# Loading the queries' input in eight strided transfers in place of one, in a cached attention block

## The chip, the cores and the metric

The kernel runs on one core of a Trainium2 chip. The metric is the device time of one execution in microseconds; of several runs the median is given. A profile is one further execution, recorded instruction by instruction: its span runs from the first to the last recorded instruction, and its own device time is a little more than the span. A core has five instruction streams: TensorE (PE, whose weight loads are listed as PEld), VectorE (DVE), ScalarE (ACT), GpSimd (POOL) and SyncE (SP). SP computes nothing; it issues nearly all transfers between the device's memory and the on-chip memory. Sixteen DMA engines carry these out.

## The reference

A block of grouped-query attention with cached keys and values: 8 sequences (B), 4 new tokens each (Sq), 32 query heads in 8 groups that share a key and value head each, 2048 cached positions (Sk), head size 128, all in bf16.

```python
def reference(x, k_cache, v_cache, wq, wo):      # x: 8 x 4 x 512
    q = (x @ wq).reshape(B, Sq, Hq, Dh).transpose(0, 2, 1, 3)
    k = jnp.repeat(k_cache, rep, axis=1)         # caches: 8 x 8 x 2048 x 128
    v = jnp.repeat(v_cache, rep, axis=1)
    scores = jnp.einsum("bhqd,bhkd->bhqk", q, k) * (Dh ** -0.5)
    p = softmax(scores)
    o = jnp.einsum("bhqk,bhkd->bhqd", p, v)
    return o.transpose(0, 2, 1, 3).reshape(B, Sq, Hq * Dh) @ wo
```

x is 32 rows of 512 numbers, 32 KB in all; each cache is 32 MB, wq and wo 4 MB each.

## The kernel before

The caches are worked through in 16 units (NU) of four key heads of one sequence. A unit has a load of keys and one of values, 2 MB each, called K0 to K15 and V0 to V15 here (load_k, line 87; load_v, line 98; V15 is cut in two). Keys and values have three buffers each (KB and VB). So K3 can only be issued when the first keys have been used, that is turned by VectorE (turn_keys, line 136), and V3 when the first values have been multiplied on TensorE (values, line 290). The output weights wo follow the last values in six pieces (load_wo, line 103), in the buffer that held wq.

All these transfers are issued by SP, in the order in which the code names them: K0 (line 105), wq (line 106), x (line 107), then K1, K2, V0 by load_ready(0, 0), and inside the loop over the units K3, V1, K4, V2 and so on, each once its buffer is free. SP works through its instructions one by one: one that waits holds up all that stand behind it.

The framework that builds the program gives each transfer a semaphore that counts its completion. For transfers issued by SP and ACT there are eight of these, used in turn; they are called lanes 0 to 7 here. Where a lane has been used before and its earlier transfer isn't yet known to SP to have landed, the framework has SP wait for that before it issues the next one on the lane. In the kernel before, the lanes of the first issues are K0 0, wq 1, x 2, K1 3, K2 4, V0 5, K3 6, V1 7, and K4 starts again with lane 0. K3 waits for lane 0, since its buffer is that of K0.

Ahead of the loop x is turned by four transposes on TensorE (line 146, out of x_sb, into xtp) and copied (line 149); 16 matmuls with wq give the queries of the first half of the heads (line 156), which are scaled (line 167), turned (line 176) and spread into the block-diagonal q_bd (line 182). Line 130 and the two turnings of K0 (line 136) stand ahead of that on VectorE and don't need x.

A pass n of the loop turns the keys of unit n (not for n = 0, done ahead), multiplies them with q_bd (scores, line 205), spreads the probabilities of unit n-1 (lines 251 to 261), takes maxima (line 223) and exponentials (line 241) of unit n, and multiplies the probabilities of unit n-2 with its values (line 290). VectorE's order is written out by hand: the turning of K1 comes behind the maxima of unit 0, and so behind all work on x. At the end, the last products with wo (project, line 358) wait for the last piece of wo, and the output is copied and sent out by ACT and SP (lines 420 to 422).

Of the kernel before, what the change touches and what calls it, by code (L numbers as in the profile page):

```python
# [14 lines left out]
def kernel(  # L15
# [9 lines left out]
    nc = tc.nc  # L25
# [42 lines left out]
    x_sb = const.tile([T, D], BF16, name="x_sb")  # L68
# [35 lines left out]

    load_k(0)
    nc.sync.dma_start(wq_sb[:, :, :], wq.rearrange("(p r) n -> p r n", r=R))
    nc.sync.dma_start(x_sb[:, :], x.flatten_outer_dims())
    loads = [("k", 1)]
    for u in range(2, NU + 2):
        if u < NU:  # L110
# [342 lines left out]
```

## Time and profile before

| | us |
|---|---|
| median of 3 runs | 185.89 (185.8 to 186.16) |
| the profiled execution, device time | 185.75 |
| the profiled execution, span | 183.8 |
| busy in the span: PE / DVE / ACT / POOL | 122.7 / 119.6 / 77.6 / 59.1 |
| HBM read | 75.53 MB, 411 GB/s over the span |
| chain that ended last: DMA / DVE / PE | 59% / 25% / 9% |

The profile's page cuts the span into 40 slices of 4.6 us and prints for each the busy share of the engines and of the DMA engines in tenths, and the bytes moved. Its chain that ended last starts from the last instruction and goes back, at each step, to what released it. Its DMA rows give, for each group of issues, the size and the median time from the start of the issue on SP to landing. Views of the trace behind the page show the same for a tile, a line or a window of time; a window that holds one issue alone gives that issue's own time to landing. SP's rows in a timeline are the issues themselves, with the time that the issuing instruction took.

### The profile page before, as it was taken

The page shows a single profiled execution, that of the slowest core. Times are in us where ns is not written, and L with a number is a line of the kernel's source. Part 1 is how long each engine was busy: PE and PEld are TensorE (multiplying, and loading weights), DVE is VectorE, ACT ScalarE, POOL GpSimd, SP SyncE. Part 2 cuts the span into 40 slices and gives each one's busy share as a digit, 9 for nine tenths or more (in the row PEclk, how much of TensorE's full clock was granted, in tenths as well). Part 3 has the DMA queues.
Part 4 walks back from the last instruction along what each step waited for, and adds up shares of the span by engine and source line. Part 5 has one row for each costly group of instructions (what it writes and reads, how often), then busy time and mean ns, then how long its engine had stood idle before and what let it go on. Part 6 is the DMA issues. An engine that isn't in the chain of part 4 may idle for free.

```text
span 183.8 us, 2500 instructions
## 1 busy us (share of the span) xinstructions
PE 122.7 (67%) x932; PEld 79.6 (43%) x932; DVE 119.6 (65%) x156; ACT 77.6 (42%) x136; POOL 59.1 (32%) x127
## 2 busy tenths in 40 slices
PE   0000471639997887849596839496866987499982
PEld 0000130214664663626364625355553746269761
DVE  4180209796999989494958677676957695945210
ACT  2000203535575764907273634538382629084020
POOL 8800111515185351605151513233231405056000
PEclk9999998556999999997969987969997599969999
DMA  6999999999999999999999999999999999999980
GB/s 193 485 399 410 428 431 431 424 442 431 428 428 435 426 421 431 428 442 431 421 435 424 431 428 431 435 428 442 417 435 421 435 435 431 431 417 424 430 353 23
DMA packets 5914, 75.71 MB, mean 412 GB/s; under 512 B 688, under 2 KB 912, under 8 KB 1296
## 3 DMA queue, kind: packets, MB, share of 16 engines
q1 hardware_dynamic: 5856, 75.55, 96.8%
q8 instruction: 7, 0.11, 0.2%
q10 hardware_dynamic: 48, 0.02, 0.0%
q14 instruction: 3, 0.02, 0.0%
HBM read 75.53 MB, written 0.03 MB: 411 GB/s over the span
## 4 chain that ended last, share of the span: by engine, by line
DMA 59%; DVE 25%; PE 9%; SPq 2%; issue 1%; POOL 1%; ACT 1%
DMA k_sb<-in_k_cache_dram 39%; DVE kt L136 19%; DMA wo_sb<-in_wo_dram 11%; DMA x_sb<-in_x_dram 9%; PE s_ps L205 5%; DVE top L223 3%; PE o_ps L290 2%; PE psq L156 1%; SPq L98 1%; DVE swapped L215 1%; POOL q_bd L182 1%; DVE q_t L176 1%; SPq L103 1%; PE out_ps L358 1%; DVE less L229 1%
## 5 line engine op out<-in xcount | busy, mean ns | idle before, releaser
L136 DVE STREAM_TRANSPOSE kt<-k_sb 128x2048 f32<-128x2048 f32 x32 | 72.0, 2288 | 21.5 <-DMA k_sb<-in_k_cache_dram 21.5
L205 PE MATMUL s_ps<-kt,q_bd 128*64 128x512 bf16 x256 | 45.0, 483 | 38.5 <-DVE kt L136 35.4
L290 PE MATMUL o_ps<-v_sb,probs 128*128 128x256 bf16 x512 | 62.9, 285 | 0.0
L261 ACT COPY probs<-p_t 32x512 bf16<-32x512 bf16 x62 | 38.2, 615 | 54.6 <-DVE r_sb L279 53.4
L261 POOL COPY probs<-p_t 32x512 bf16<-32x512 bf16 x63 | 38.5, 612 | 58.8 <-DVE r_sb L279 56.4
L290 PEld LDWEIGHTS <-probs 128*128 128x128 bf16 x512 | 51.2, 102 | 14.5 <-issue 6.6
L205 PEld LDWEIGHTS <-q_bd 128*64 128x64 bf16 x256 | 17.1, 127 | 56.3 <-issue 24.7
L223 DVE TENSOR_REDUCE top<-s_ps 128x1 f32<-128x1024 f32 x16 | 19.6, 1223 | 16.1 <-PE s_ps L205 16.1
L241 ACT ACTIVATE s_sb<-s_ps,less 128x1024 bf16<-128x1024 f32 x16 | 22.3, 1397 | 10.6 <-DVE less L229 10.2
L215 POOL COPY l_swapped<-l_sb 64x1 f32<-64x1 f32 x32 | 5.8, 180 | 32.1 <-ACT s_sb L241 31.3
L306 ACT ACTIVATE o_sc<-o_ps,r_sb 64x128 f32<-64x128 f32 x28 | 10.1, 362 | 7.4 <-PE o_ps L290 6.7
L146 PE MATMUL xtp<-ident,x_sb 32*128 32x32 bf16 x4 | 0.3, 194 | 18.3 <-DMA x_sb<-in_x_dram 18.3
L251 DVE STREAM_TRANSPOSE p_t<-s_sb 128x512 f32<-128x512 f32 x16 | 11.0, 689 | 1.6 <-ACT s_sb L241 1.6
L167 ACT ACTIVATE q_nat<-psq 128x512 bf16<-128x512 f32 x2 | 1.2, 590 | 18.8 <-PE psq L156 18.8
L182 POOL COPY q_bd<-q_t 32x512 bf16<-32x512 bf16 x6 | 3.7, 624 | 16.6 <-DVE q_t L176 16.5
L313 PEld LDWEIGHTS o_t<-both,o_sc 128*128 128x128 f32 x32 | 5.2, 204 | 6.8 <-issue 5.1
L146 PEld LDWEIGHTS <-x_sb 32*128 32x128 bf16 x4 | 0.2, 113 | 18.3 <-DMA x_sb<-in_x_dram 18.3
L313 PE MATMUL o_t<-both,o_sc 128*128 128x64 f32 x32 | 7.2, 311 | 0.2 <-DVE o_sc L308 0.2
L129 POOL MEMSET probs<- 128x4096 bf16 x2 | 7.0, 3512 | 0.0
L215 DVE COPY swapped<-top 64x1 f32<-64x1 f32 x32 | 4.7, 148 | 0.8
L358 PE MATMUL out_ps<-wo_sb,oP 128*32 128x256 bf16 x64 | 4.6, 274 | 0.5 <-DMA wo_sb<-in_wo_dram 0.5
L308 DVE TENSOR_SCALAR o_sc<-o_ps,r_sb 64x128 f32<-64x128 f32 x4 | 1.4, 349 | 4.7 <-issue 3.0
(32 smaller groups left out, 39.3 us busy)
## 6 DMA issues: line engine op xcount, KB each, us to landing
k_sb<-in_k_cache_dram SPq DMA_DIRECT2D x16, 2048.0 KB, 24.6
v_sb<-in_v_cache_dram SPq DMA_DIRECT2D x15, 2048.0 KB, 23.5
wq_sb<-in_wq_dram SPq DMA_DIRECT2D x1, 4096.0 KB, 16.9
wo_sb<-in_wo_dram SPq DMA_DIRECT2D x3, 1024.0 KB, 17.6
v_sb<-in_v_cache_dram SPq DMA_DIRECT2D x1, 1536.0 KB, 13.9
wo_sb<-in_wo_dram SPq DMA_DIRECT2D x1, 640.0 KB, 20.6
v_sb<-in_v_cache_dram SPq DMA_DIRECT2D x1, 512.0 KB, 14.8
wo_sb<-in_wo_dram SPq DMA_DIRECT2D x1, 256.0 KB, 19.2
```

The lines of the kernel that those rows point to most:

```text
L129: nc.gpsimd.memset(pr[:, :, :, :, :, :], 0.0)
L136: nc.vector.transpose(kts[(u, t)][:, :, :, :, :].rearrange("k c h s e -> k (c h s e)").bitcast(FP32), ks[u][:, t * CT : (t + 1) * CT, :].r ...
L205: nc.tensor.matmul(s_pss[u][h * NQ : (h + 1) * NQ, t, :, :], lhsT=q_bd[:, hq, k, e, b, :, :].rearrange("k g q -> k (g q)"), rhs=kts[(u, t) ...
L215: engine.tensor_copy(out=out[h * NQ : (h + 1) * NQ, :], in_=in_[(1 - h) * NQ : (2 - h) * NQ, :])
L223: nc.vector.reduce_max(out=top[:, :], in_=s_pss[u][:, :, :, :].rearrange("q t c s -> q (t c s)"), axis=AX,)
L241: nc.scalar.activation(out=s_sbs[u][:, :, :, :].rearrange("q a s j -> q a j s"), in_=s_pss[u][:, :, :, :].rearrange("q t (a j) s -> q (t a ...
L251: nc.vector.transpose(p_t[:, :, :, :, :].rearrange("s x g q j -> s (x g q j)").bitcast(FP32), s_sbs[u][:, :, :, :].rearrange("q a s j -> q ...
L261: by[h * G + g](out=probs[u % PB][g * S : (g + 1) * S, h, :, :, g, :], in_=p_t[quad * S : (quad + 1) * S, :, g % 2, :, :].rearrange("s x q ...
L290: nc.tensor.matmul(o_pss[u][:, :, :].rearrange("n j d -> n (j d)"), lhsT=probs[u % PB][:, h, t * CT // 4 + a, :, :, :].rearrange("s j g q ...
L306: nc.scalar.mul(out=to, in_=of, mul=by)
L313: nc.tensor.matmul(o_t[:, :], lhsT=o_scs[u][:, :], rhs=both[:, :], start=True, stop=True)
L358: nc.tensor.matmul(out_ps[half * T : (half + 1) * T, :], lhsT=oP[p // 2][:, r, p % 2, :], rhs=wo_sb[:, p * WR + r, half * DH : (half + 1) ...
```

## The change

In place of one transfer of 32 rows there are eight of four rows each: transfer i takes rows i, i+8, i+16 and i+24 of x, to the partitions of the same numbers. All are issued by SP at the place of the one before, ahead of K1. A row is 1 KB, a transfer 4 KB. The lines below it in the file move down by one.

```diff
     load_k(0)
     nc.sync.dma_start(wq_sb[:, :, :], wq.rearrange("(p r) n -> p r n", r=R))
-    nc.sync.dma_start(x_sb[:, :], x.flatten_outer_dims())
+    for i in range(8):
+        nc.sync.dma_start(x_sb[i::8, :], x.flatten_outer_dims()[i::8, :])
     loads = [("k", 1)]
```

In the program as built, the orders of PE, DVE, ACT and POOL are the same as before; SP's has seven more issues. The first transpose on TensorE (line 147 now) waits on eight lanes in place of one.

## The prediction

> **What bounds the kernel now.** I read the page first, for which resource has no slack:
>
> ```profile
> span 183.8 us, 2500 instructions
> ...
> DMA  6999999999999999999999999999999999999980
> GB/s 193 485 399 410 428 431 431 424 442 431 428 428 435 426 421 431 428 442 431 421 435 424 431 428 431 435 428 442 417 435 421 435 435 431 431 417 424 430 353 23
> ```
>
> The transfers are never idle between the first slice and the last two, and their rate hardly moves. The table by stage (columns: window, its length, busy time of PE, PEld, DVE, ACT and POOL with counts, TensorE clock, DMA share, GB/s) says it more sharply:
>
> ```profile
> 18.00:60.00 42.00, 28.11 (x196) 14.86 (x197) 30.40 (x39) 17.73 (x30) 14.57 (x33) 0.84 1.01 431
> 60.00:100.00 40.00, 30.30 (x226) 20.10 (x226) 31.11 (x42) 21.59 (x38) 13.49 (x33) 0.91 1.01 429
> 100.00:140.00 40.00, 29.57 (x226) 19.56 (x223) 29.41 (x37) 19.90 (x36) 11.88 (x28) 0.91 1.01 430
> 140.00:179.00 39.00, 33.42 (x274) 24.27 (x275) 22.17 (x37) 16.69 (x31) 11.16 (x24) 0.87 1.00 422
> ```
>
> Every compute engine has slack in each stage; the DMA share is full at some 430 GB/s. So the stream of loads sets the end, and a hole made in it moves the end by the length of the hole. Next, who feeds it: SP's timeline (start, time, what).
>
> ```profile
> 0.74 0.38 SPq L87 DMA_DIRECT2D k_sb<-in_k_cache_dram  x1
> 1.17 0.42 SPq L106 DMA_DIRECT2D wq_sb<-in_wq_dram  x1
> 1.64 0.42 SPq L107 DMA_DIRECT2D x_sb<-in_x_dram  x1
> 2.11 0.99 SPq L87 DMA_DIRECT2D k_sb<-in_k_cache_dram  x2
> 3.15 0.44 SPq L98 DMA_DIRECT2D v_sb<-in_v_cache_dram  x1
> 12.92 0.33 SPq L87 DMA_DIRECT2D k_sb<-in_k_cache_dram  x1
> 13.29 0.43 SPq L98 DMA_DIRECT2D v_sb<-in_v_cache_dram  x1
> 33.62 0.33 SPq L87 DMA_DIRECT2D k_sb<-in_k_cache_dram  x1
> ```
>
> K1, K2 and V0 are issued by 3.6 us, long before K0, wq and x have landed. The issue rows (last column: issue to landing) time those:
>
> ```profile
> wq_sb<-in_wq_dram SPq DMA_DIRECT2D x1, 4096.0 KB, 16.9
> ...
> x_sb<-in_x_dram SPq DMA_DIRECT2D x1, 32.0 KB, 16.6
> out_dram<-out_sb SPq DMA_DIRECT2D x1, 16.0 KB, 1.4
> out_dram<-out_sb ACTq DMA_DIRECT2D x1, 16.0 KB, 1.6
> ```
>
> wq lands at 1.17 + 16.9 = 18.07 us, x at 1.64 + 16.6 = 18.2. The view of k_sb, narrowed to single issues, gives the landings of K0 (issued at 0.74), K1 (at 2.11) and K4 (at 33.62):
>
> ```profile
> DMA to landing us min/median/max: 7.6/7.6/7.6
> ```
> ```profile
> DMA to landing us min/median/max: 20.9/20.9/20.9
> ```
> ```profile
> DMA to landing us min/median/max: 13.6/13.6/13.6
> ```
>
> K1 lands at 23.0. The same view gives K2 2.6 + 25.2 = 27.8, V0 3.15 + 29.6 = 32.75, K3 12.9 + 24.7 = 37.6, V1 13.3 + 29.1 = 42.4 and K4 47.2: one every 4.85 us, without a hole. From K1's landing to the last weights (20.63 us after 158.56 in the chain of waits, 179.2) the stream carries 30 more 2 MB loads and 4 MB of wo, as much as 32 loads; 32 x 4.85 = 155.2 of the 156.2 us that pass. So at most 1 us of idle lies in it that could swallow a delay.
>
> **The change, part by part.** It removes one issue of 32 rows and adds eight of four; nothing else moves on any engine. But the built program takes its transfers' completion semaphores from eight lanes in turn, and a transfer on a used lane waits until the transfer before it on that lane has landed. Its SP order now reads:
>
> ```
> k_sb      (lane 0)      wq_sb (lane 1)
> x_sb x6   (lanes 2 to 7)
> x_sb      waits lane 0  (K0 landed)
> x_sb      waits lane 1  (wq landed)
> k_sb K1   waits lane 2  (first x piece)
> k_sb K2   waits lane 3;  v_sb V0 waits lane 4;  K3 lane 5;  V1 lane 6
> ```
>
> Step 1, the first six pieces: 6 x 0.42 (the x row) plus gaps of 0.05 from 1.64, so to about 4.5. Cost nothing: K0 and wq, 16 us of transfers, lie ahead; without that cover it would be 6 x 0.47 = 2.8.
>
> Step 2, the seventh waits for K0 and goes out at 0.74 + 7.6 = 8.35. Nothing, under the same cover. Behind it on SP stand the eighth piece and all of K1, K2, V0, K3, V1.
>
> Step 3, the eighth waits for wq at 18.07; with 0.05 of gap and 0.42 of issue SP is free at 18.54, and K1 is issued at about 18.6 in place of 2.11. By then every transfer issued has landed: the stream is dry. (The first x piece, K1's own wait, stood directly behind wq, as x did, 18.2.)
>
> Step 4, K1 restarts it. No row of before shows a 2 MB load into an idle stream in mid-run, so I bound it. Upper: K0's 7.6 us, same size, idle stream. Lower: 4.85 of steady transfer plus the 1.4 that a tiny transfer (out_dram) takes from issue to landing, 6.25. K0 is the nearest row, but it stands at the program's start, so I take the middle, 6.95, and keep both ends. K1 lands at 18.6 + 6.95 = 25.5, +2.5 us (bounds +1.85 and +3.2). A fit of a Trainium skill page (DMA: Bandwidth & Descriptors, Anatomy of one DMA: some 2 us fixed plus bytes at 436 GB/s, measured for transfers issued from GpSimd) would give 6.8 and a sum of +2.4; no row here shows that path.
>
> Step 5, x itself. The eighth piece, issued at 18.12, lands 1.4 to 1.6 later (the out_dram rows): 19.5 to 19.7, +1.3 to +1.5 on line 146 and on everything up to the first turning of K1 at 29.1 (there in before). I add nothing for it: compute runs behind its loads there (K1 at 25.5 for use at about 30.5, K2 at 30.3 for 38.8). TensorE's one wait on x becomes eight, seven already met.
>
> Step 6, is the hole filled later, or a second one opened? The stretch in which compute paces the issues is to 65 us. K4, the thinnest, lands 13.6 after issue, 4.85 of it its own: 8.7 us of queue ahead. After the change its issue is 1.4 later and the queue 2.5 later, so this grows. K2, V0, K3 and V1 follow K1 at some 0.45 each, against 4.85 of transfer each. Neither.
>
> Sum: 0 + 0 + 2.5 + 0 = +2.5 on the profiled execution's 185.75 us, 188.3; its span would be 186.3. The median of the runs is 185.89, 0.14 above it, which I don't add.
>
> **The rivals.** (a) *Only x's lateness counts.* The printed chain runs from x through DVE's work to 65.05 before it becomes K and wo loads; taken literally, the end moves with x: +1.3 to +1.5, 187.15. For it: the chain. Against: at 65.05 the step is a K load of 22.3 us, 17 of it spent behind other loads, so the start of that wait sets nothing.
>
> (b) *Not slower.* The place is the eighth piece's wait on wq's lane. Were it met early, as by counts of other transfers or of rings that finish first, K1 would join a stream that still runs: an issue before 23.0 - 7.6 = 15.4 lands K1 no later than now. Then the pieces cost nothing and x, still behind wq, gains nothing: 185.75. Against: in before SP's waits for landings (14.0 us on K loads) are really spent.
>
> (c) *The small transfers cost by themselves.* A page's rule speaks against this change: pieces under 64 KB are mostly overhead and should be one transfer (Trainium skill, DMA: Bandwidth & Descriptors, Rules for kernel authors). As a mechanism: if each of seven more pieces held up the stream for the 1.4 us of an out_dram row, +9.8, 195.55. Against: x's 32 KB, queued behind wq, landed 0.2 us after it. By that rule 195.55, by the row at most 7 x 0.2.
>
> **How the numbers follow.** Forecast 188.3, chance 0.80; (a) 0.09; (b) 0.06; (c) 0.02; the rest, 0.03, for a restart outside both bounds or something unseen. Range 187.0 to 189.3: the restart's bounds give 187.6 to 189.0; below it reaches to take in (a), above it leaves 0.3 for issues of pieces longer than x's row. A change under 0.2% (0.37 us) can't be told from none here: same 0.05, from (b); faster 0.03, the rest of (b) and half of the remainder; slower 0.92.
>
> **What would show it.** On SP: six issues of x by 4.5, one at 8.4, one at about 18.1, K1 at 18.6, then K2 to V1 in a row to about 21. The GB/s row has a dip near 18 to 20 us and is as before elsewhere. K1 needs 6.25 to 7.6 from issue to landing. L146 starts at 19.5 to 19.7. All later landings, the last wo's at 179.2 among them, are some 2.5 later. I am wrong if x's last issue comes before 15, if K1's landing moves while the last wo's doesn't, or if an engine, not a load, is what the last projections wait for.

## The result and the profile after

| | before | after |
|---|---|---|
| median of 6 runs, us | 185.95 (185.78 to 186.16) | 189.12 (188.72 to 189.23) |
| ratio | | 1.0168, 95% interval 1.0156 to 1.0181 |
| profiled execution: device time / span | 185.75 / 183.8 | 189.23 / 187.1 |

In later runs some executions were disturbed and some per cent longer; medians and ratios leave these out, and each experiment is given by its ratio to the kernel before on the same chip.

The page of the changed kernel, first its span and the two rows of the transfers in 40 slices:

```profile
span 187.1 us, 2511 instructions
...
DMA  6996799999999999999999999999999999999991
GB/s 182 483 420 265 236 434 427 434 438 420 427 434 427 434 422 429 433 431 431 424 441 424 427 441 420 431 438 427 427 431 441 420 427 445 417 428 417 430 379 40
```

The fourth and fifth slices (14 to 23 us) have 265 and 236 GB/s, where the kernel before had 410 and 428. From the sixth on the rows are as before. A table by windows of 1 us (columns as in the prediction; the last two are DMA share and GB/s) shows the hole itself. It counts a packet, whole, in the window in which the packet starts:

```profile
16.00:17.00 1.00, 0.00 (x0) 0.00 (x0) 0.00 (x0) 0.00 (x0) 0.00 (x0) 1.00 1.06 459
17.00:18.00 1.00, 0.00 (x0) 0.00 (x0) 0.00 (x0) 0.00 (x0) 0.00 (x0) 1.00 0.09 24
18.00:19.00 1.00, 0.00 (x0) 0.00 (x0) 0.00 (x0) 0.00 (x0) 0.00 (x0) 1.00 0.02 5
19.00:20.00 1.00, 0.00 (x0) 0.00 (x0) 0.00 (x0) 0.00 (x0) 0.00 (x0) 1.00 0.08 20
20.00:21.00 1.00, 0.53 (x8) 0.34 (x12) 0.22 (x1) 0.00 (x0) 0.00 (x0) 1.00 1.30 262
21.00:22.00 1.00, 1.00 (x12) 0.31 (x8) 0.00 (x0) 0.00 (x0) 0.00 (x0) 1.00 0.63 229
22.00:23.00 1.00, 0.64 (x8) 0.00 (x0) 0.00 (x0) 0.30 (x1) 0.00 (x0) 1.00 1.00 426
```

Next to nothing starts from 17 to 20 us, and two more microseconds pass at little more than half the rate before the stream is full again. By the packets' own records wq's last ones run on until 17.83 us and K1's first starts at 19.99; the few in between belong to x. K1's packets that start by 21.2 us take 0.67 to 1.98 us each, those of the full stream 0.61. Who left the stream empty stands in SP's waits (total, times, longest), and SP's timeline has what came after:

```profile
SPq L108 <- DMA wq_sb<-in_wq_dram: 9.2, 1, 9.2
...
SPq L108 <- DMA k_sb<-in_k_cache_dram: 3.0, 1, 3.0
```
```profile
8.52 10.33 SPq L108 DMA_DIRECT2D x_sb<-in_x_dram  x2
18.89 0.91 SPq L87 DMA_DIRECT2D k_sb<-in_k_cache_dram  x2
```

The seventh piece waited 3.0 us for K0, the eighth 9.2 us for wq, and K1 went out at 18.89 in place of 2.11. The chain that ended last now starts with wq, and ends as it did:

```profile
1.20 17.06 DMA wq_sb<-in_wq_dram
18.27 1.79 DMA x_sb<-in_x_dram
...
161.99 20.80 DMA wo_sb<-in_wo_dram
182.83 1.34 PE out_ps L359 x16
```

The eighth piece is issued at 18.27, at once when wq has landed, and lands 1.79 later. The trace keeps completion marks for each lane: one each time that a part of a transfer reports its end, sixteen for a whole load. By the last of these marks, K1 has landed at 26.60 (22.96 before) and the last piece of wo at 183.83 (180.17 before): +3.64 and +3.66. What was lost by 26.6 us was neither made up nor added to. The span grew by 3.3, not 3.66; the missing 0.33 lies behind the output and is taken up below.

### The profile page after: what moved, and what is told of

Its sections match the earlier page's. It is cut to its first block, busy times and chain, and to the rows that moved or that the text cites. A ratio compares the mean times of both kernels' runs of the same rounds, so it can differ in the third digit from the quotient of the medians.

```text
span 187.1 us, 2511 instructions
## 1 busy us (share of the span) xinstructions
PE 123.7 (66%) x932; PEld 79.7 (43%) x932; DVE 119.7 (64%) x156; ACT 77.6 (41%) x136; POOL 59.4 (32%) x127
## 4 chain that ended last, share of the span: by engine, by line
DMA 61%; DVE 24%; PE 10%; SPq 1%; issue 1%; POOL 1%; ACT 1%
DMA k_sb<-in_k_cache_dram 39%; DVE kt L137 18%; DMA wo_sb<-in_wo_dram 11%; DMA wq_sb<-in_wq_dram 9%; PE s_ps L206 6%; DVE top L224 3%; PE o_ps L291 2%; PE psq L157 1%; DMA x_sb<-in_x_dram 1%; DVE swapped L216 1%; POOL q_bd L183 1%; DVE q_t L177 1%; PE out_ps L359 1%; SPq L103 1%; DVE less L230 1%
## 5 line engine op out<-in xcount | busy, mean ns | idle before, releaser
L206 PE MATMUL s_ps<-kt,q_bd 128*64 128x512 bf16 x256 | 46.6, 497 | 38.6 <-DVE kt L137 35.7
L291 PE MATMUL o_ps<-v_sb,probs 128*128 128x256 bf16 x512 | 61.7, 281 | 0.0
L291 PEld LDWEIGHTS <-probs 128*128 128x128 bf16 x512 | 50.5, 101 | 13.8 <-issue 6.6
L206 PEld LDWEIGHTS <-q_bd 128*64 128x64 bf16 x256 | 17.4, 130 | 57.1 <-issue 26.6
L314 PEld LDWEIGHTS o_t<-both,o_sc 128*128 128x128 f32 x32 | 5.7, 224 | 7.6 <-issue 5.8
L314 PE MATMUL o_t<-both,o_sc 128*128 128x64 f32 x32 | 7.9, 336 | 0.2 <-DVE o_sc L309 0.2
```

The costliest lines, as they stand in the source:

```text
L206: nc.tensor.matmul(s_pss[u][h * NQ : (h + 1) * NQ, t, :, :], lhsT=q_bd[:, hq, k, e, b, :, :].rearrange("k g q -> k (g q)"), rhs=kts[(u, t) ...
L291: nc.tensor.matmul(o_pss[u][:, :, :].rearrange("n j d -> n (j d)"), lhsT=probs[u % PB][:, h, t * CT // 4 + a, :, :, :].rearrange("s j g q ...
L314: nc.tensor.matmul(o_t[:, :], lhsT=o_scs[u][:, :], rhs=both[:, :], start=True, stop=True)
```

## Experiments

Theory W: SP, held by the wait on wq's lane, lets the stream run dry. Theory P: the small transfers cost the time by themselves. The edits are shown against the kernel before, except where an edit of the changed kernel is named.

| kernel | ratio to before | 95% interval |
|---|---|---|
| six pieces | 0.9977; again 0.9975 | 0.9965 to 0.9989; 0.996 to 0.999 |
| seven pieces | 1.0123 | 1.0093 to 1.0153 |
| the wait alone | 1.0148 | 1.0130 to 1.0166 |
| wq behind six pieces | 1.0054 | 1.0038 to 1.0069 |
| x behind K1 | 1.0011 | 0.9985 to 1.0037 |
| eight blocks | 1.0144; again 1.0146 | 1.0124 to 1.0164; 1.0121 to 1.017 |
| eight columns | 1.0142 | 1.0122 to 1.0162 |
| the changed kernel again | 1.0175 | 1.0152 to 1.0197 |
| eight pieces from ACT | 1.0120 | 1.0098 to 1.0141 |
| five values cut | 0.9985 | 0.9969 to 1.0001 |

### How many pieces

```diff
-    nc.sync.dma_start(x_sb[:, :], x.flatten_outer_dims())
+    for i in range(6):      # the other kernel: 7
+        nc.sync.dma_start(x_sb[i::6, :], x.flatten_outer_dims()[i::6, :])
```

> x in six pieces (rows i, i+6, ...), so that K1 waits only for K0's lane and K2 for wq's. Theory W (SP's wait for wq lets the stream of loads run dry): K1 is issued at about 8.5 us, behind wq, the stream has K1 to carry when wq lands, nothing is lost: 185.9, within 0.4. Theory P (the small transfers themselves hold the stream up): six of eight pieces cost six eighths of the 3.2 us measured with eight: 188.3.

> x in seven pieces, so that K1 itself waits for wq's lane. Theory W: the stream runs dry again, K1 is issued at about 18.1 in place of 18.9 (no eighth piece to issue ahead of it), lands at about 25.8: 2.4 to 2.9 us over the kernel before, 188.3 to 188.8. Theory P: seven eighths of 3.2: 188.7. What tells the two apart is the step from six to seven pieces: W 2.4 or more, P 0.4.

Six pieces cost nothing, seven 1.2%: medians 185.43 and 188.08. Both lie a little under what W named (185.5 and 188.3 at the least); from the output's landing to the end 0.37 and 0.44 us less pass than in the kernel before, which is taken up below. Theory P has no place for such a step. SP's timeline with six pieces shows why it is there:

```profile
1.64 4.47 SPq L108 DMA_DIRECT2D x_sb<-in_x_dram  x6
8.71 10.11 SPq L87 DMA_DIRECT2D k_sb<-in_k_cache_dram  x2
18.86 0.43 SPq L98 DMA_DIRECT2D v_sb<-in_v_cache_dram  x1
```

Now it is K2 that waits for wq (K1 and K2 together take 10.11 us), but K1 was issued at 8.71 and lies behind wq in the stream, so there is work for the DMA engines when wq is done. With seven pieces K1 itself waits, goes out at 18.27, and the hole is back. One piece more or less decides, since it decides which transfer meets wq's lane.

### The wait without the pieces

```diff
         ks[u] = kpool.tile([128, C, Dh], BF16, tag="k_sb", name="k_sb")
+        if u == 1:
+            nc.scalar.copy(out=ks[u][0:1, 0, 0:2], in_=wq_sb[0:1, 0, 0:2])
```

> x in one transfer as before; K1 alone is held back until wq has landed, by a copy of two numbers of wq on ACT into K1's buffer that K1 then overwrites. Theory W: K1 is issued at about 18.4, lands 7.7 later at 26.1, and the end moves by about 3.1: 188.7 to 189.1. Theory P: no small pieces, so 185.9.

The median was 188.69, the ratio 1.0148: most of the change's 1.0168 with no small transfer in the kernel. SP's timeline, and the time from K1's issue to its landing:

```profile
18.39 0.81 SPq L89 DMA_DIRECT2D k_sb<-in_k_cache_dram  x2
```
```profile
DMA to landing us min/median/max: 7.7/7.7/7.7
```

K1 takes 7.7 us into a dry stream, as K0 did at the program's start (7.6). It goes out 0.5 us earlier here than in the changed kernel (18.39 for 18.89), with no eighth piece to issue ahead of it.

### The pieces without the wait

This is an edit of the changed kernel: wq stands behind six pieces of x, and no issue meets its lane at the start.

```diff
-    nc.sync.dma_start(wq_sb[:, :, :], wq.rearrange("(p r) n -> p r n", r=R))
     for i in range(8):
+        if i == 6:
+            nc.sync.dma_start(wq_sb[:, :, :], wq.rearrange("(p r) n -> p r n", r=R))
         nc.sync.dma_start(x_sb[i::8, :], x.flatten_outer_dims()[i::8, :])
```

> All eight small pieces are kept, but wq is issued behind the first six, so that no issue waits for wq: the seventh waits for K0, the eighth and K1 for early pieces, all landed by about 9 us. Theory W: K1 is issued at about 10 us, far ahead of the stream's need: 185.9 to 186.5. Theory P: the pieces are all there: 189.1.

The ratio of 1.0054 is some 1 us in place of 3.2; the median, 186.83, is 0.3 above what W named. K1 goes out at 9.80 and there is no hole like the changed kernel's, but the pieces aren't free here. Each strided piece has four late marks where a whole load has sixteen, which I read as four of the DMA engines. The six pieces, queued between K0 and wq, land 0.18 us apart (8.35, 8.53, 8.71, 8.90 and so on). From 7.75 to 8.5 us the packet records show some 13 packets under way at a time, where the kernel before has 16. wq's last mark comes at 19.34, where it was at 18.05 in the kernel before: +1.3, about the 6 x 0.18 = 1.1 of the pieces. The last piece of wo lands 1.3 later too (181.44 for 180.17). So in this place I put the pieces at about 0.2 us each. That is no price of small pieces in every running stream: in the kernel with six pieces they stand between wq and K1, land some 0.2 us apart too, and the last piece of wo lands at 180.18, as in the kernel before. Why they cost time ahead of wq and none behind it, no run here shows. In the changed kernel they stand at the edge of the hole.

### Does x's lateness count?

```diff
+    load_k(1)
     nc.sync.dma_start(x_sb[:, :], x.flatten_outer_dims())
-    loads = [("k", 1)]
+    loads = []
```

> x in one transfer, but behind K1 in place of ahead of it, so that it lands about 4.9 us later (near 23.1) while the stream of loads stays full. Theory W (the loads set the end, x's lateness nothing): 185.9 within 0.5. Rival, that the printed chain is to be taken literally and the end moves with x: 185.9 + 4.9 = 190.8.

The ratio was 1.0011, and its interval includes 1. TensorE's first transpose started at 23.38 us, 5.1 later than before, and the end hardly moved: the interval's upper end allows 0.7 us, where the rival named 4.9. The chain of the kernel before, which leads from x to 65 us, was no measure of x's price.

### How the rows are cut

```diff
-    nc.sync.dma_start(x_sb[:, :], x.flatten_outer_dims())
+    for i in range(0, T, 4):          # blocks
+        nc.sync.dma_start(x_sb[i : i + 4, :], x.flatten_outer_dims()[i : i + 4, :])
+    for i in range(0, D, 64):         # columns (the other kernel)
+        nc.sync.dma_start(x_sb[:, i : i + 64], x.flatten_outer_dims()[:, i : i + 64])
```

> Eight pieces of four rows that lie side by side (rows 0 to 3, 4 to 7, ...), with the same order and waits. Theories W and P: 189.1 as with the strided pieces, within 0.3. A third theory, that the step of eight partitions costs something: 186 to 188.5.

> Eight pieces of all 32 rows and 64 columns each, 128 bytes a row, with the same order and waits as the changed kernel. Theory W: 189.1 within 0.4, since K1 waits for the same landing. Theory P: the cost hangs on how a piece lies on the DMA engines (other rings, 32 short rows in place of four long), so it moves by more than 0.5 from 189.1.

Blocks and columns both came to 188.5 (188.51, 188.44), 0.6 under the changed kernel. Both miss what W named (within 0.3 and 0.4 of 189.1), and columns moved by a little more than the 0.5 that P named. But they moved down, and some 2.6 of the 3.2 us stay however the rows are cut, which speaks for W; the 0.6 had to be looked at on one chip:

> The changed kernel once more, on the chip of the three runs below. 189.1 within 0.4.

> Eight pieces of four neighbouring rows, beside the changed kernel on one chip. If the step of eight partitions costs the issue itself (the trace has 0.576 us for a strided issue, 0.295 for a block), K1 goes out 0.2 to 0.4 earlier and the time is 0.3 to 0.6 under the changed kernel's. If the difference of the first two runs (188.5 against 189.1) was the chip's, the two are equal within 0.2.

188.99 against 188.46: again 0.5 apart. The intervals of the two ratios overlap, so these are two like results rather than a firm one, but the issues have a cause to show. The view of x_sb for the changed kernel, the blocks and the columns (ns, least, median, greatest; first and last start):

```profile
L108 SPq DMA_DIRECT2D x_sb<-in_x_dram x8: 576/576/736, 1.7 to 18.3; - x8
```
```profile
L108 SPq DMA_DIRECT2D x_sb<-in_x_dram x8: 247/295/376, 1.6 to 18.4; - x8
```
```profile
L108 SPq DMA_DIRECT2D x_sb<-in_x_dram x8: 311/422/545, 1.6 to 18.0; - x8
```

An issue of four partitions eight apart takes SP 0.576 us, of four neighbouring ones 0.295. Seven of the eight are hidden; the eighth stands between wq's landing and K1. K1 is issued at 18.89 and 18.75 in the two profiles of the changed kernel, at 18.66 and 18.46 with blocks: 0.2 to 0.3 of the 0.5. The rest I can't place. With columns K1 goes out at 18.38, 0.5 earlier than in the changed kernel's first profile; half of that is wq, which landed at 18.01 there and at 18.26 with the strided pieces.

### The pieces on another queue

This too is an edit of the changed kernel.

```diff
-        nc.sync.dma_start(x_sb[i::8, :], x.flatten_outer_dims()[i::8, :])
+        nc.scalar.dma_start(x_sb[i::8, :], x.flatten_outer_dims()[i::8, :])
```

> The eight strided pieces are issued by ACT, which does nothing until 18 us, in place of SP. In the built program the eighth then waits for K0 alone, wq waits for the first piece and K1 for the second, which land in the first few us. Theory W (SP held until wq lands, stream dry): wq and K1 go out within 8 us, the stream stays full: 185.6 to 187.0, the upper part if small pieces hold up four rings by 0.18 us each beside a running load. Theory P: 189.1, the pieces are all there.

The ratio was 1.0120, the median 187.95, outside what either theory named, because I had misread which lane is whose: with x on ACT's queue the first piece takes lane 0 and K0 lane 1, so wq, the next on lane 1, waits for K0. The chain of waits says so:

```profile
0.74 7.75 DMA k_sb<-in_k_cache_dram
8.51 12.11 DMA wq_sb<-in_wq_dram
```

wq goes out only when K0 has landed, into a dry stream, and lands at 20.6 in place of 18.05. The hole is of the same kind and merely stands at another place: the last piece of wo is 2.6 late (182.75). As a mend this failed; as a test it shows that a dry stream costs its price with another pair of transfers too.

### The end, and why six pieces beat the kernel before

> Six pieces again, since the first run of it came out under the kernel before. If that is real, it comes from the end: SP's closing waits go through the lanes in a fixed order, the output's lane stands last in it with six pieces and first in the kernel before, and 0.93 us in place of 1.30 pass between the output's landing and the end: 185.5 to 185.7, ratio 0.997 to 0.999. If it was chance: 185.9, ratio 1.000.

The gain is there again, 0.25%. The issue of the output by SP, in the kernel before, in the changed one and with six pieces (first run):

```profile
180.93 0.35 SPq L422 DMA_DIRECT2D out_dram<-out_sb  x1
```
```profile
184.59 0.36 SPq L423 DMA_DIRECT2D out_dram<-out_sb  x1
```
```profile
180.93 0.36 SPq L423 DMA_DIRECT2D out_dram<-out_sb  x1
```

With spans of 183.8, 187.1 and 183.5, about 2.9, 2.5 and 2.6 us follow that issue. The trace's records of SP's closing waits show them in pairs of semaphores, in a fixed order. In the kernel before the output's two transfers hold lanes 2 and 1, whose pairs come first and second; three more pairs follow after the output has landed. With eight pieces they hold lanes 1 and 0 (second and third), with six lanes 7 and 6, whose pairs come last. From the output's last mark to the end 1.30 us pass in the kernel before, 0.97 with eight pieces, 0.93 with six. The pairs that follow the landing make little of that, at some 0.07 us each. Most of it is one later instruction of SP, recorded as DRAIN: it starts 0.47 us after the one ahead of it in the kernel before, 0.09 with eight and with six pieces. To turn the lanes as far as six pieces do without touching x:

```diff
         cuts = [0, C] if u < NU - 1 else [0, 3 * C // 4, C]
+        if 3 <= u < 8:
+            cuts = [0, C // 2, C]
```

> x in one transfer as in the kernel before; five value loads in the middle (V3 to V7) are each cut into two halves, so that the lanes turn five places further and the output's two transfers get lanes 6 and 7, as with six pieces. If the gain of six pieces comes from where the output's lanes stand in SP's closing waits: about 0.93 us from the output's landing to the end in place of 1.30, 185.5 to 185.7, ratio 0.997 to 0.999. If it comes from the pieces of x: 185.9, ratio 1.000. If halves of loads or their lane waits cost something: above 185.9.

From the output's last mark to the end 0.94 us pass here too, with x in one transfer, and the DRAIN comes 0.09 after the instruction ahead: a shorter closing needs no pieces of x. All profiles fit with the lanes: 1.30 or 1.31 us where the output holds lanes 1 and 2 (the kernel before, the wait alone, x behind K1), 0.86 to 0.97 in all others. But those three are also the ones with 43 transfers in all, the others with 48 to 50, so that it is the lanes and not the number is not shown. The ratio, 0.9985 (0.9969 to 1.0001), points the same way but can't be told from 1. That six pieces of x are faster by 0.2% is measured twice. It doesn't come from an earlier x, which lands later (line 147 starts at 19.57, where line 146 started at 18.28); the shorter closing is the one gain that the traces show.

## Why the prediction was right, and where it was off

**What bounds the kernel**, right. A delay of 3.64 us in K1's landing came out as 3.66 in the last weights' landing, through 157 us of loads at the same rate. One reading on the way was off: 179.2 is the landing of the fourth of six pieces of wo, and the last one landed at 180.17. So 155.2 of 157.2 us were taken, and 2 us of idle, not 1, could have swallowed a delay; they swallowed none.

**Steps 1 and 2**, right in cost. The issues took 0.576 in place of 0.42 each, under cover; the seventh went out at 8.52 (8.35 foretold).

**Step 3**, right, and 0.3 short. K1 was issued at 18.89 for 18.6: wq's landing let SP go at 18.27 rather than 18.12, and the eighth issue took 0.58 rather than 0.42. That every transfer had landed by then was not quite so: by the completion marks pieces three to seven landed at 18.80 to 19.53, one every 0.18. With the wait alone, without pieces, K1 took as long to land, so this cost next to nothing.

**Step 4** is the term that was mis-sized. I took 6.95 us for K1 into a dry stream, the middle between K0's row and a steady transfer with a tiny one's latency; it took 7.71 (26.60 - 18.89), just above the upper bound of 7.6. The nearest row, K0's, was right, and discounting it for standing at the program's start was not: a dry stream starts slowly in mid-run too, as the window from 21 to 22 us with its 229 GB/s and K1's first packets show. The estimate of 6.8 us from the fit in the Trainium skill (DMA: Bandwidth & Descriptors, Anatomy of one DMA), which is given there for transfers issued from GpSimd, missed by more; the measurement decides.

**Step 5**, right in what it costs. x was later than foretold (line 147 at 20.12, not 19.5 to 19.7): the last piece was issued 0.15 later and took 1.79 to land, not the 1.4 to 1.6 of the output's rows. With x 5.1 us late in an experiment the end stayed where it was.

**Step 6**, right: K4 was issued at 35.36, 1.74 later than before, and the rate has no second hole.

**What the sum left out**: the closing, 0.33 shorter. So 2.5 became 2.5 + 0.3 + 0.76 - 0.33 = 3.2, where 3.3 was measured in the spans and 3.2 in the medians. That the time fell inside the range owes something to luck: 189.12 is above the 189.0 to which the restart's bounds led and 0.2 under the range's end of 189.3. With a closing as long as before it would have been some 189.45, outside.

**The rivals.** (a) fell with x behind K1. (b) didn't happen: SP waited its 9.2 us. (c) isn't the cause: the wait alone costs most of the time with no small transfer in the kernel. The pieces cost about 0.2 us each ahead of wq and nothing behind it, in no place the 1.4 of the rival.

## What to carry to other kernels

Count the transfers in flight against the semaphores that the framework has for them: the issue that comes round to a lane waits for that lane's last transfer, and if that is the longest one in the queue and nothing else has been issued behind it, the stream runs dry. Read the waits in the built order of the issuing queue, not in the source; one small transfer more or less can move a large load onto the wrong lane. A stream that has run dry costs its gap and a slow start besides: counted from its issue, the first 2 MB load took some 2.8 us more here than the 4.85 of a steady one.

## What the hardware showed that I had not expected

- A restart in mid-run is as slow as the first load: 7.7 us for 2 MB at 18.9 us, 7.6 at 0.7 us, against 4.85 in the stream. In all seven profiles in which K1 met a dry stream it took 7.57 to 7.80.
- Small transfers queued on the same DMA engines land 0.18 us apart, although a packet of theirs is recorded with 0.046 us; with six of them ahead of wq its last mark came 1.3 us later, with six behind it the end didn't move.
- SP's issue of four rows takes 0.295 us for neighbouring partitions and 0.576 for partitions eight apart; that of all 32 in one took 0.42.
